# A gated linear attention with an expert layer: split first queries, one span turned by transfers, stores on two queues, and a new hand-written order

## The chip, the cores and the metric

The kernel runs on one core of a Trainium2 chip. The metric is device time in microseconds of one execution. Engines in the profile: PE (TensorE), DVE (VectorE), ACT (ScalarE), POOL (GpSimd) and SP (SyncE), which in the kernel before issues all transfers.

## The reference

```python
def _attn_ref(q, k, v, f_logit):            # each (4, 8, 768, 48)
    f = 1.0 / (1.0 + np.exp(-f_logit))
    for t in range(S):
        state = f[:, :, t, :, None] * state + np.einsum('bhd,bhe->bhde', k[:, :, t], v[:, :, t])
        y[:, :, t] = np.einsum('bhd,bhde->bhe', q[:, :, t], state)
    return y

def _moe_ref(x, w1, w2, w_out):             # x: (3072, 384), d_ff = 1024
    g = np.maximum(x @ w1, x @ w2)
    return g @ w_out
```

`y`, with the heads side by side, is the `x` of the second function. All inputs and the output are float32.

## The kernel before

**Tiling.** The 768 positions of each of 4 batches are cut into 3 windows of 256. A *span* is one window of one batch; spans 0 to 3 are the first windows, 4 to 7 the second, 8 to 11 the third. So span s needs the state that span s−4 left. A tile of an input holds one span: 128 rows, and in each row two neighbouring positions (even, odd) of all 8 heads. Each span has two halves of 64 rows, h = 0 and 1, one after the other in time.

**Work of one span.** Every step is a letter. Loads: `Lf`, `Lq`, `Lk`, `Lv`, into one of 27 `slots` (the number behind @). ScalarE makes the gates: `E`, `F` (exp and ln of the gate's input), `G`; `e` adds the two logs of a row, `C` sums them along the rows on TensorE, `Z` and `X` take exp of the sums (`dec`, `inv`). `i` and `j` put the odd gate into the even keys and queries; `K`, `Q`, `V` write scaled keys, queries and values as bf16 (`kp`, `qp`, `vb`). `t` and `u` turn keys and queries on TensorE (16 transposes each into PSUM, the queries' beside the keys'), and `U` copies the turned ones out to `trs`. `A` (two parts) multiplies turned keys and queries, `m` applies the mask while copying (`at_m`), `D` makes the state's addition, `n` and `N` update the state. `S` (two parts) adds what the old state gives to the output's banks, `y` what the masked products give; `z` is a small copy that stands between the two. `Y` copies the result out: as `xT` (features on the partitions) for most spans; for the spans in `TURNED` (6 to 10) rows stay on the partitions (`xr`, a single buffer), and `M`, a transposing transfer on SyncE's queue, makes `xT`.

**Expert layer.** max(h1, h2) = relu(h1 − h2) + h2. So `wd` = w1 − w2 (`ws`, four quarters of columns), and m2 = w2 · w_out is made once on the chip (`wc` casts w2, `wt` transposes it, `wx` copies it out, `wo` casts w_out, `wm` multiplies, `wn` copies out). `Wa`, `Wb`, `Wo` load quarters of w1, rows of w2, halves of w_out. Then for each span: `d` (four parts, 6 matmuls each) gives `wd`·x, `r` copies it with relu to `gT`, `o` (two parts by parity; three in span 11) adds m2·x (3 matmuls) and w_out·gT (8), `b` copies the result to `ob` (three buffers), `O` stores it.

**The order.** There is no scheduler at run time: the string `ORDER` is read word by word and each word calls one step. A word is the letter, the span (with the part after a point), the engine (a, v, p or s) and, behind @, a PSUM bank or a slot. Each engine runs its own instructions in this order, and waits at each for what it needs; what stands behind a waiting instruction on the same engine waits too. Up to eight transfers are in flight: the ninth is issued when the first has landed, since its semaphore is used again. Numbers such as L436 are lines of the kernel before: L114 is the helper `copy` that all plain copies share, L436 the matmuls of `d`, L461 of `o`, L292 of `A`, L387 of `D`, L314 and L323 of `S` and `y`, L503 the m2 product, L275 the transposes, L299 `m`, L261 `Q`, L258 `K`, L247 `i`, L251 `j`, L224 `e`, L511 `ws`, L404 and L406 `n`, L357 `z`, L213 `E`, L125 the input loads, L427 `M`, L475 to L482 the stores.

Of the kernel before, what the change touches and what calls it, by code (L numbers as in the profile page):

```python
# [12 lines left out]
BF16 = mybir.dt.bfloat16  # L13
# [10 lines left out]
n0.1v D1@0 m0.0v@4 S0.0@2 A1.0@6 Lk2s@25 wc2a z0v@2 m1.0v@6 A1.1@4 S0.1 y0 Lq2s@26 wc0a ws2p n1.0v  # L24
n1.1v m1.1v@4 S1.0@6 Y0.0a@2 wt2@0 Lf3s@16 E2 g5p z1v@6 N1.1v S1.1 y1 N0.1p Lv2s@17 g3p ws0v wt0@1
Y1.1a@7 wx2a@0 Y0.1v@3 wc1p Lq3s@18 Y1.0v@6 d0.2@2 F2 g1p ws3v d0.0@4 Lk3s@19 wx0a@1 wt1@0 g4v e2v
d0.3@3 ws1v C2@1 r0.1a@2 d1.2@6 Lf4s@21 wo0v wx1v@0 wo1p d0.1@5 G2 d1.3@7 r0.0v@4 d1.0@2 Lv3s@20
wo2p wo3a d1.1@3 r1.1v@6 Z2 wm0@0 X2 g6v Lk4s@22 r1.0a@2 i2v wm1@1 K2v Lf5s@23 j2v wm2@2 Q2v Lq4s@24
E3 wn1v@1 t2@4 u2@4 F3 U2.0v@4 Lf6s@12 V2p wn2a@2 wn0v@0 o0.1@1 U2.1v@5 e3p A2.1@2 Lq5s@13 b0.1.0a@1
D2@4 A2.0@6 G3 n2.0v C3@0 j3v o1.1@1 Z3 n2.1v Lk5s@0 i3v X3 Q3v o1.0@0 m2.1v@2 E4 K3p F4 m2.0v@6  # L30
# [18 lines left out]
r7.0a@4 N9.0v i10p Lv10s@24 d8.3@7 O6.2s X10 d8.1@5 r7.1a@2 K10v d8.2@6 d8.0@4 r8.1a@6 o7.1@1
r8.0a@4 j10v Q10p S9.0@2 t11@4 t10@6 z9v@2 u11@4 S9.1 y9 U11.0v@4 u10@6 U11.1v@5 o7.0@0 U10.2a@6  # L50
V11v V10v b7.1.0v@1 o8.1@4 Y9.2a@2 b7.0.0a@0 M9s D10@1 b8.1.0a@4 D11@0 O7.2s A11.0@2 A10.0@6 n11.0v
A11.1@4 m10.0v@6 o8.0@0 m11.1v@4 d9.0@6 N11.0v n10.0v d9.1@7 m11.0v@2 N10.0p d9.3@5 r9.0a@6 d9.2@4
b8.0.0v@0 O8.2s S10.0@0 r9.1a@4 S11.0@2 z10v@0 A10.1@6 z11v@2 S11.1 y11 m10.1v@6 S10.1 y10 Y11.0a@2
Y11.1a@3 o9.0@4 Y10.2a@0 M10s d11.2@5 b9.0.0v@4 d11.1@0 d11.3@1 o9.1@4 d10.1@3 b9.1.0v@4 r11.4a@5
# [7 lines left out]
TURNED = (6, 7, 8, 9, 10)  # L62


@with_exitstack
def kernel(
# [255 lines left out]
    def add_turned(s, h, n, lhs, rhs, stop):  # L322
        nc.tensor.matmul(out=banks[:, ys[s] + h, n * D:(n + 1) * D], lhsT=lhs, rhs=rhs,  # L323
                         start=(s, h) not in begun, stop=stop, skip_group_check=True)
        begun.add((s, h))

    def step_S(s, part, b):
        t = tr[s]
        if s in TURNED:
            ys[s] = b if part == 0 else ys[s]  # L330
            for j in range(NP):
# [242 lines left out]
```

## Time and profile before

| | us |
|---|---|
| median of 3 runs (139.22 to 140.53) | 140.16 |
| the profiled execution | 141.23 |
| span of the profiled execution, first to last instruction | 139.5 |
| PE busy | 119.1 |
| DVE busy | 101.7 |
| ACT busy | 79.0 |
| POOL busy | 45.3 |

In the profile, a row of an engine's time line is its start, its length, the engine, the line, the operation with the tiles it writes and reads, how many of them follow each other, and in brackets the idle time before it with what ended that. The granted clock of TensorE is given as 1.00 over the whole span. 23.59 MB are read from memory and 4.72 MB written.

### The profile page before, as it was taken

Reading aid. Unit: us, or ns where it says so; the run is one execution under the profiler, and the core shown is the slowest. Engines: PE = TensorE matmul, PEld = TensorE weight load, DVE = VectorE, ACT = ScalarE, POOL = GpSimd, SP = SyncE. Lnnn points to the kernel's source line nnn. Section 1 sums busy time; section 2 is a strip of 40 time slices with the busy share of each in tenths; the row PEclk is TensorE's granted clock in tenths of the full one; section 3 lists DMA queues with packets and bytes.
Section 4 is the critical chain, followed back from the end, with each engine's and each line's share of the span. In section 5 each row is a group of like instructions: output and inputs, shape, how many; then the busy total and the mean of one; then the engine's idle time right before and its main releaser. Section 6 shows DMA issues by size and latency. Waiting matters only on the chain. (4 is left out here: it accounts for less than half of the span.)

```text
span 139.5 us, 5551 instructions
## 1 busy us (share of the span) xinstructions
PE 119.1 (85%) x2455; PEld 89.5 (64%) x2455; DVE 101.7 (73%) x173; ACT 79.0 (57%) x120; POOL 45.3 (32%) x52
## 2 busy tenths in 40 slices
PE   0045489599999999999999699989999999999991
PEld 0024377586567687677787566776877668778671
DVE  5687798999889999989974989982642768312630
ACT  3784349665592996973983355693675814504301
POOL 5003007640538224482073096719635001000000
PEclk9999999999999999999999999999999999999999
DMA  4999999999999989999999999909899461422124
GB/s 109 271 261 296 348 332 349 369 267 251 269 265 257 271 222 273 239 248 250 247 297 222 224 274 163 288 30 96 121 260 313 130 140 34 118 56 61 57 62 164
DMA packets 59768, 29.65 MB, mean 213 GB/s; under 512 B 54368, under 2 KB 58592, under 8 KB 59744
## 3 DMA queue, kind: packets, MB, share of 16 engines
q1 hardware_dynamic: 59744, 29.30, 87.5%
q8 instruction: 19, 0.31, 1.0%
q14 instruction: 5, 0.04, 0.1%
HBM read 23.59 MB, written 4.72 MB: 203 GB/s over the span
## 5 line engine op out<-in xcount | busy, mean ns | idle before, releaser
L436 PE MATMUL banks<-xT,wd 128*128 128x256 bf16 x288 | 34.7, 273 | 2.3 <-DVE xT L114 2.0
L461 PE MATMUL banks<-wo,gT 128*128 128x384 bf16 (+1 forms) x200 | 35.3, 320 | 0.0
L436 PEld LDWEIGHTS <-wd 128*128 128x128 bf16 x288 | 27.2, 98 | 6.9 <-issue 2.3
L445 ACT ACTIVATE gT<-banks 128x1024 bf16<-128x1024 f32 (+1 forms) x20 | 19.5, 982 | 20.2 <-PE banks L436 15.7
L299 DVE TENSOR_TENSOR at_m<-banks,mask 128x1024 bf16<-128x1024 f32 x24 | 28.8, 1218 | 0.8 <-PE banks L292 0.5
L461 PEld LDWEIGHTS <-gT 128*128 128x128 bf16 x200 | 19.2, 98 | 11.8
L247 POOL TENSOR_TENSOR slots<-slots,one 128x384 f32<-128x384 f32 x8 | 8.5, 1058 | 28.1 <-DMA slots<-in_k_dram 18.3
L461 PE MATMUL banks<-m,xT 128*128 128x384 bf16 (+1 forms) x75 | 15.9, 320 | 0.0
L114 ACT COPY ob<-banks 128x384 f32<-128x384 f32 (+1 forms) x16 | 7.4, 460 | 11.9 <-PE banks L461 11.9
L114 DVE COPY trs<-banks 128x2048 bf16<-128x2048 bf16 (+1 forms) x12 | 11.9, 997 | 2.4 <-PE banks L275 2.3
L213 ACT ACTIVATE gate<-slots 128x768 f32<-128x768 f32 x12 | 10.1, 841 | 5.0 <-DMA slots<-in_f_logit_dram 5.0
L114 DVE COPY ob<-banks 128x384 f32<-128x384 f32 x9 | 5.0, 555 | 8.9 <-PE banks L461 8.9
L228 PE MATMUL banks<-e,u_inc 128*128 128x384 bf16 x12 | 4.2, 354 | 8.0 <-DVE e L224 8.0
L258 POOL TENSOR_TENSOR kp<-slots,inv 128x768 bf16<-128x768 f32 x5 | 9.6, 1913 | 3.0 <-DVE slots L247 2.9
L404 DVE TENSOR_TENSOR tmp_s<-banks,state 128x192 f32<-128x192 f32 x16 | 5.6, 352 | 6.7 <-ACT ob L114 3.9
L217 ACT ACTIVATE ell<-gate 128x768 f32<-128x768 f32 x12 | 10.1, 845 | 0.2
L292 PE MATMUL banks<-trs 48*64 48x128 bf16 x384 | 10.1, 234 | 0.0
L261 POOL TENSOR_TENSOR qp<-slots,dec 128x768 bf16<-128x768 f32 x4 | 7.3, 1817 | 8.3 <-PE banks L314 4.9
L251 DVE SCALAR_TENSOR_TENSOR slots<-gate,slots 128x384 f32<-128x384 f32 x12 | 6.6, 552 | 3.9 <-DMA slots<-in_q_dram 3.9
L114 ACT COPY trs<-banks 128x1024 bf16<-128x1024 bf16 (+1 forms) x4 | 4.8, 1227 | 7.0 <-PE banks L275 7.0
L292 PEld LDWEIGHTS <-trs 48*64 48x64 bf16 x384 | 7.5, 115 | 1.6 <-issue 1.1
L461 PEld LDWEIGHTS <-xT 128*128 128x128 bf16 x75 | 6.5, 97 | 3.2
(73 smaller groups left out, 186.3 us busy)
## 6 DMA issues: line engine op xcount, KB each, us to landing
slots<-in_f_logit_dram SPq DMA_DIRECT2D x12, 384.0 KB, 6.4
slots<-in_q_dram SPq DMA_DIRECT2D x12, 384.0 KB, 6.2
slots<-in_k_dram SPq DMA_DIRECT2D x12, 384.0 KB, 6.1
slots<-in_v_dram SPq DMA_DIRECT2D x12, 384.0 KB, 5.8
out_dram<-ob SPq DMA_DIRECT2D x6, 384.0 KB, 3.9
out_dram<-ob SPq DMA_DIRECT2D x11, 192.0 KB, 3.4
slots<-in_moe_w_dram SPq DMA_DIRECT2D x4, 384.0 KB, 8.7
slots<-in_moe_w_dram SPq DMA_DIRECT2D x3, 512.0 KB, 8.8
```

Source lines behind the costliest of these rows:

```text
L114: (nc.scalar.copy if e == "a" else engines[e].tensor_copy)(out, in_)
L213: nc.scalar.activation(flat(gate[s]), flat(loaded[s]["f"]), AF.Exp, bias=0.0, scale=-1.0)
L217: nc.scalar.activation(flat(ell[s]), flat(gate[s]), AF.Ln, bias=1.0, scale=1.0)
L247: engines[e].tensor_mul(even, even, one[s])
L251: engines[e].scalar_tensor_tensor(out=even, in0=gate[s][:, :, 1, :], scalar=1.0, in1=even, op0=ALU.add, op1=ALU.mult)
L258: engines[e].tensor_mul(pad("kp", s)[:, :, :, 0:D], by_parity(loaded[s]["k"]), both(inv[s]))
L261: engines[e].tensor_mul(pad("qp", s)[:, :, :, 0:D], by_parity(loaded[s]["q"]), both(dec[s][:, 0:HD].rearrange("p (h d) -> p h d", h=H)))
L292: nc.tensor.matmul(out=ps[h * HC:(h + 1) * HC, j % 2, par, :], lhsT=t[rows, h, 0, j, par, :], rhs=t[rows, h, 1, j].rearrange("p a t -> p ( ...
L299: nc.vector.tensor_mul(at[s][:, jj].rearrange("p r j a t -> p (r j) (a t)"), banks[:, b:b + 2, :].rearrange("p r (j x) -> p (r j) x", j=2) ...
L436: nc.tensor.matmul(out=ps[:, f], lhsT=wd[:, kt, ff * C:(ff + 1) * C], rhs=xT[g][:, kt], start=(kt == 0), stop=(kt == KT - 1))
L445: nc.scalar.activation(dst, src, AF.Relu)
L461: nc.tensor.matmul(out=ps, lhsT=lhs, rhs=rhs, start=(i == 0), stop=(i == len(terms) - 1))
```

## The change

It has four parts.

- The queries of spans 0 and 1 are scaled in two halves of four heads (`q0.0`, `q0.1`), transposed in two halves (`uq`), and copied to `trs` in two halves (`U` parts 4 and 5), apart from the keys (part 3).
- Span 11 (`BY_DMA`) has no transposes and no `U`: two transposing transfers on SyncE's queue (`Mk`, `Mq`) write `trs` straight from `kp` and `qp`, in another layout, and `A` and `S` read it through `key_t` and `query_t`. The branch for such spans inside `step_S` under `TURNED` isn't reached, as 11 is not in `TURNED`.
- `O` takes an engine. The stores of spans 7, 8, 9 and the last one of span 11 (seven transfers) are issued from ScalarE's queue, the others from SyncE's as before.
- `ORDER` is written anew from the first word to the last: order of loads, engines of many steps, banks and slots.

```diff
-Lf0s@16 g0v Lf1s@17 Lq0s@18 Lk0s@19 Lk1s@20 Lv0s@21 Lq1s@22 Wa2s E0 Wb1s F0 Lv1s@23 E1 e0v C0@0 F1
-Wb2s j0v Z0 e1v X0 Q0v G0 C1@1 Wb0s i0v X1 u0@2 G1 g2v K0v Lf2s@24 i1p t0@2 U0.0v@2 U0.1a@3 Wa0s V0v
-Z1 K1v D0@2 A0.1@0 Wa3s j1v A0.0@4 Q1v Wa1s m0.1v@0 u1@6 t1@6 Wo0s n0.0v U1.0a@6 U1.1a@7 Wo1s V1v
...
+Lf0s@16 g5p g7v g3v Lf1s@17 g2p Lk0s@18 g0p Wb2s Lq0s@19 Lq1s@20 Lv0s@21 Lf2s@22 E0 Wb0s F0 Wb1s E1
+e0v C0@0 F1 Lk1s@23 G0 X0 i0v G1 Wa1s wc2v Z0 K0v e1v Wa0s t0@0 j0v wt2@2 U0.3v@0 Lv1s@24 q0.0v C1@3
+j1v uq0.0@0 q0.1v Wa3s V0v uq0.1@0 U0.5a@0 wx2v@2 U0.4a@0 A0.1@4 Z1 Wa2s A0.0@0 m0.1v@4 X1 q1.0p E2
+Wo1s g6p q1.1v m0.0v@0 g4p uq1.1@2 uq1.0@2 U1.5a@2 wc0p D0@4 Lf3s@25 F2 n0.0v S0.0@0 Wo0s z0v@0 i1p
+n0.1v S0.1 y0 N0.1p Lq2s@26 K1v wt0@4 Y0.1a@1 wc1a U1.4v@2 ws1v t1@2 wt1@5 U1.3a@2 e2v Lk2s@16 ws0v
+C2@6 wx0a@4 A1.1@2 Y0.0v@0 Lv2s@17 V1p wx1v@5 d0.0@0 m1.1v@2 d0.1@1 Lk3s@18 ws3p A1.0@4 r0.0a@0 D1@2
+m1.0v@4 Lq3s@19 Z2 ws2p d0.3@1 G2 n1.0v X2 n1.1v S1.0@4 z1v@4 S1.1 y1 Lv3s@21 wo2v d0.2@0 Y1.0v@4
...
+j11v Z10 K10v C11@3 b6.0.0v@4 V9v Y8.2a@0 d7.3@7 d7.2@6 Z11 M8s b6.1.0a@2 Q11v d7.0@0 X11 r7.1a@6
+d7.1@1 K11p Mq11s D9@2 r7.0a@0 A9.1@4 A9.0@6 o7.0@3 O4.2s j10v Mk11s m9.1v@4 Q10p d8.3@1 O6.2s
+m9.0v@6 d8.2@0 d8.0@4 n9.0v r8.1a@0 N9.0p d8.1@5 S9.0@0 r8.0a@4 u10@6 t10@6 z9v@0 V11v S9.1 y9
+U10.2a@6 o7.1@2 Y9.2v@0 M9s b7.0.0a@3 A10.1@0 b7.1.0v@2 D11@3 A11.1@4 O5.2s A10.0@6 n11.0v O7.2a
...
 TURNED = (6, 7, 8, 9, 10)
+BY_DMA = (11,)
...
+    def step_q(s, jj, e):
+        hs = slice(4 * jj, 4 * jj + 4)
+        sums = dec[s][:, 0:HD].rearrange("p (h d) -> p h d", h=H)[:, hs]
+        engines[e].tensor_mul(pad("qp", s)[:, :, hs, 0:D], by_parity(loaded[s]["q"])[:, :, hs],
+                              sums.unsqueeze(1).to_broadcast([C, 2, 4, D]))
...
-    def transposes(s, x, b):
+    def transposes(s, x, b, js=range(NP)):
         src = pad("kpqp"[2 * x:2 * x + 2], s)
-        for j in range(NP):
+        for j in js:
...
     def step_U(s, part, e, b):
         t = tr[s] = buf("trs", s, 3, [C, 2, 2, NP, 2, HC], BF16)
+        if part > 2:
+            x, js = (0, slice(0, NP)) if part == 3 else (1, slice(2 * part - 8, 2 * part - 6))
+            src = banks16[:, b:b + 2, :].rearrange("p h (x j y) -> p h x j y", x=2, j=NP)
+            copy(e, t[:, :, x, js].rearrange("p h j a t -> p h (j a t)"),
+                 src[:, :, x, js].rearrange("p h j y -> p h (j y)"))
+            return
...
+    def whole(t):
+        return t.rearrange("p h x j a t -> p (h x j a t)").rearrange("p (x k c) -> p x k c", x=2, k=2 * NP)
+
+    def step_turn(s, x, e):
+        t = tr[s] = buf("trs", s, 3, [C, 2, 2, NP, 2, HC], BF16)
+        src = pad("kpqp"[2 * x:2 * x + 2], s).rearrange("p two h e -> p (two h e)")
+        engines[e].dma_start(out=whole(t)[:, x], in_=src, transpose=True)
+
+    def key_t(s, rows, h, j, par):
+        if s in BY_DMA:
+            return whole(tr[s])[rows, 0, NP * par + j, h * HC:(h + 1) * HC]
+        return tr[s][rows, h, 0, j, par, :]
+
+    def query_t(s, rows, h, j):
+        if s in BY_DMA:
+            return whole(tr[s])[:, 1].rearrange("p (a j) c -> p a j c", a=2)[rows, :, j, h * HC:(h + 1) * HC]
+        return tr[s][rows, h, 1, j]
...
-                        nc.tensor.matmul(out=ps[h * HC:(h + 1) * HC, j % 2, par, :],
-                                         lhsT=t[rows, h, 0, j, par, :],
-                                         rhs=t[rows, h, 1, j].rearrange("p a t -> p (a t)"),
-                                         start=True, stop=True, skip_group_check=True)
+                        nc.tensor.matmul(out=ps[h * HC:(h + 1) * HC, j % 2, par], lhsT=key_t(s, rows, h, j, par),
+                                         rhs=query_t(s, rows, h, j), start=True, stop=True, skip_group_check=True)
...
-    def step_O(g, part):
+    def step_O(g, part, e):
...
-                nc.sync.dma_start(out=dst[a], in_=obs[g][a * HC:(a + 1) * HC])
+                engines[e].dma_start(out=dst[a], in_=obs[g][a * HC:(a + 1) * HC])
...
+        "uq": lambda s, i, e, b: transposes(s, 1, b, range(2 * i, 2 * i + 2)),
+        "q": lambda s, i, e, b: step_q(s, i, e),
...
+        "Mk": lambda s, e, b: step_turn(s, 0, e), "Mq": lambda s, e, b: step_turn(s, 1, e),
```

More of the change, by code (lines that the diff above doesn't have):

```diff
@@ L26 @@
[L26 to L30, printed above, removed]
@@ L49 @@
[L49 to L54, printed above, removed]
@@ L346, in step_S @@
                     add(s, h, 2 * j + r, state_before(s, h)[rows].rearrange("p x e -> p (x e)"),
[L347 removed]
+                        D + ZP * j, query_t(s, rows, h, j), False)
     def step_z(s, b):
```

74 lines of the change are left out of this document (42 added, 32 removed).

## Prediction

> **What bounds the kernel now.** I read the page first, then a table of four stretches, then the time line of the start engine by engine, then the groups of instructions, last the transfers.
>
> ```profile
> span 139.5 us, 5551 instructions
> PE 119.1 (85%) x2455; PEld 89.5 (64%) x2455; DVE 101.7 (73%) x173; ACT 79.0 (57%) x120; POOL 45.3 (32%) x52
> ...
> DMA  4999999999999989999999999909899461422124
> ```
> ```profile
> core 0: us, PE busy (x) PEld busy (x) DVE busy (x) ACT busy (x) POOL busy (x), PEclk, DMA share, GB/s
> 0.00:25.80 25.80, 10.95 (x338) 9.39 (x338) 20.41 (x50) 15.28 (x22) 7.02 (x17) 1.00 1.07 285
> 25.80:36.30 10.50, 10.47 (x117) 8.13 (x117) 10.22 (x15) 6.53 (x11) 2.68 (x5) 1.00 1.08 283
> 36.30:136.60 100.30, 97.67 (x2008) 71.96 (x2000) 71.04 (x109) 56.84 (x91) 35.56 (x32) 1.00 0.83 189
> 136.60:139.50 2.90, 0.00 (x0) 0.00 (x0) 0.00 (x0) 0.31 (x1) 0.00 (x0) 1.00 0.36 129
> ```
>
> The reader is to see three parts. Until 25.8 us TensorE has work for 10.95 us only, while the transfers run without a break (share 1.07). From 25.8 to 136.6 us TensorE stands idle for 0.03 + 2.63 us in all: it sets the time there. The tail, 2.9 us, is the last copy and the last store. So a change can win at most about 2.7 us of idle time in the long part, what it takes off TensorE, and what it moves at the start. VectorE is the second engine to watch: 10.22 us of the 10.5 right after the start.
>
> **The start, before.** What arrives when can be read from instructions that were waiting for a transfer; they start as it lands.
>
> ```profile
> 4.45 0.84 ACT L213 ACTIVATE gate<-slots 128x768 f32<-128x768 f32 x1 [2.44 <-DMA slots<-in_f_logit_dram]
> 7.46 0.56 DVE L251 SCALAR_TENSOR_TENSOR slots<-gate,slots 128x384 f32<-128x384 f32 x1 [0.70 <-DMA slots<-in_q_dram]
> 10.60 1.15 POOL L247 TENSOR_TENSOR slots<-slots,one 128x384 f32<-128x384 f32 x1 [8.06 <-DMA slots<-in_k_dram]
> 17.37 0.56 DVE L114 CAST vb<-slots 128x768 bf16<-128x768 f32 x1 [0.81 <-DMA slots<-in_v_dram]
> 20.15 1.05 ACT L114 CAST slots<-slots 128x1024 bf16<-128x1024 f32 x1 [1.94 <-DMA slots<-in_moe_w_dram]
> 21.48 1.04 ACT L114 CAST slots<-slots 128x1024 bf16<-128x1024 f32 x1 [0.28 <-DMA slots<-in_moe_w_dram]
> 24.18 1.03 DVE L511 TENSOR_TENSOR wd<-slots 128x768 bf16<-128x768 f32 x1 [0.47 <-DMA slots<-in_moe_w_dram]
> 28.39 0.84 POOL L114 CAST wo<-slots 128x768 bf16<-128x768 f32 x1 [1.84 <-DMA slots<-in_moe_w_out_dram]
> 30.49 0.83 ACT L114 CAST wo<-slots 128x768 bf16<-128x768 f32 x1 [0.61 <-DMA slots<-in_moe_w_out_dram]
> ```
>
> The order of the loads there is f0 f1 q0 k0 k1 v0 q1 Wa2 Wb1 v1 Wb2 Wb0 f2 Wa0 Wa3 Wa1 Wo0 Wo1. They land one behind the other: f0 4.45, q0 7.46, k1 10.60, so an input tile costs about 1.5 us. Wb2 to Wb0 is 1.33 for a row block of w2. Wb0 to Wa0 (with f2) is 2.7, so a quarter of w1 is about 1.2; by 28.39 and 30.49 half of w_out is 2.1. One gap does not fit: v1 to Wb2 took 2.78 where 1.33 was due, 1.4 us more.
>
> ```profile
> 20.03 1.27 PE L314 MATMUL banks<-at_m,vb 64*64 64x128 bf16 x35
> 22.77 0.88 PE L314 MATMUL banks<-at_m,vb 64*64 64x128 bf16 x44
> 25.83 1.47 PE L436 MATMUL banks<-xT,wd 128*128 128x256 bf16 x12 [1.64 <-DVE xT L114]
> 28.51 3.43 PE L436 MATMUL banks<-xT,wd 128*128 128x256 bf16 x30
> 31.78 4.06 PE L503 MATMUL banks<-wo,slots 128*128 128x384 bf16 x24
> 35.77 0.41 PE L275 MATMUL banks<-ident,kp 64*128 64x64 bf16 x16
> 36.02 0.40 PE L275 MATMUL banks<-ident,qp 64*128 64x64 bf16 x16
> 38.24 0.43 PE L292 MATMUL banks<-trs 48*64 48x128 bf16 x16
> 38.48 0.43 PE L387 MATMUL banks<-vb,kp 64*64 64x48 bf16 x32
> ```
>
> Here TensorE takes up the expert part (d0) at 25.83, after both first spans are wholly done, and ends the product for m2 at 35.84. These two points are my marks.
>
> **The change at the start.** The new order loads f0 f1 k0 Wb2 q0 q1 v0 f2 Wb0 Wb1 k1 Wa1 Wa0 v1 Wa3 Wa2 Wo1 f3 Wo0 q2 k2 v2. With the costs above from f0 at 4.45: k0 7.4, Wb2 8.7, q0 10.2, q1 11.7, v0 13.2, f2 14.7, Wb0 16.0, Wb1 17.3, k1 18.8, Wa1 20.0, Wa0 21.2, v1 22.7, Wa3 23.9, Wa2 25.1, and Wo0 30.8, each up to 1.4 later if the unexplained gap comes back. Weights come earlier, span 1's keys 8 us later.
>
> What has to be done on VectorE is priced by these groups:
>
> ```profile
> L299 DVE TENSOR_TENSOR at_m<-banks,mask 128x1024 bf16<-128x1024 f32 x24 | 28.8, 1218 | 0.8 <-PE banks L292 0.5
> L261 DVE TENSOR_TENSOR qp<-slots,dec 128x768 bf16<-128x768 f32 x8 | 7.6, 954 | 0.2
> L258 DVE TENSOR_TENSOR kp<-slots,inv 128x768 bf16<-128x768 f32 x7 | 6.6, 945 | 1.1 <-POOL slots L247 1.0
> L224 DVE TENSOR_TENSOR e<-ell 128x384 bf16<-128x384 f32 x6 | 3.2, 541 | 0.8 <-ACT ell L217 0.8
> L511 DVE TENSOR_TENSOR wd<-slots 128x768 bf16<-128x768 f32 x3 | 2.9, 973 | 0.5 <-DMA slots<-in_moe_w_dram 0.5
> L114 DVE COPY trs<-banks 128x1024 bf16<-128x1024 bf16 x5 | 3.4, 688 | 1.5 <-PE banks L275 1.5
> L114 DVE CAST xT<-banks 128x384 bf16<-128x384 f32 x2 | 1.0, 544 | 0.0
> L404 DVE TENSOR_TENSOR tmp_s<-banks,state 128x192 f32<-128x192 f32 x16 | 5.6, 352 | 6.7 <-ACT ob L114 3.9 <-PE banks L387 2.5
> L357 DVE COPY look<-banks 128x1 f32<-128x1 f32 x4 | 0.6, 150 | 0.0
> ```
>
> The first step there that a new order can hold up is i0. It needs G0, the fifth activation on ScalarE: four of 0.84, as in the 4.45 row, and one of half the width, about 0.5, from 4.45 on, so 8.3. Then, in the order written: i0 0.54 (half a tile, as e); wc2, a cast of 1024 columns that VectorE never did before (from below the 0.69 of its 1024-column copy, from above the 1.22 of its masked product over 1024 columns; I take 1.0, near ScalarE's cast of this shape, 1.05 in the 20.15 row); K0 0.95; e1 0.54; j0 0.55; U0 0.69; q0.0 0.48; j1 0.55; q0.1 0.48; V0 0.56; wx2 0.69. That is 7.0, to 15.3. Half of Q is taken as half of 954; from below nothing is saved on it, so 0.95 at most. Then m0.1 1.22, q1.1 0.48, m0.0 1.22, n0.0 and n0.1 0.35 each, z0 0.15: 3.8, with about 1.2 of waits for TensorE between them (A0, S0), to 20.3. K1 comes next, and it is held by k1, not by VectorE: k1 at 18.8 to 20.2, then i1 on GpSimd (1.15, the 10.60 row): 20.0 to 21.4. Behind K1 stand U1 (half of 0.69, taken as 0.4), ws1 0.97, e2 0.54, ws0 0.97, Y0.0 0.54; with K1 4.4 us. So d0 can start at 24.7 to 25.8, against 25.83. That is the gain of the halves and of the earlier weights: 0 to 1.1 us.
>
> What is behind it costs more. At that point, before, span 1 was done. Now A1.0, D1, S1 and y1 are still to come: half of span 1's A (the 38.24 row less its overlap with the next) 0.3; D 0.4; S, 12 matmuls, and y1, 48, at 0.88/44 each, 1.2; in all 1.9 us of TensorE. In return wt1 and C2 are done ahead, by their columns about 0.6. And y1 waits for VectorE again: after Y0.0 come wx1 0.69, m1.1 and m1.0 2.44, n1.0 and n1.1 0.7, so 28.5 to 29.6. Until then TensorE has d0.0, d0.1, d0.3 (18 at 3.43/30, 2.06 us), A1.0, D1: 2.8 us, from 24.7, to 27.5. It idles about 1 us. After that all is dense: y1, d0.2, d1 (30 at 0.114, 3.4), the m2 product 4.06. Sum to the second mark, without C3, which is only moved: 24.7 to 25.8, plus d0 and d1 5.5, plus span 1's 1.9, plus 1.0 idle, plus 3.95 = 37.1 to 38.2. Before it was 35.84. **The start loses 1.3 to 2.3 us; I take 1.6**, nearer the lower end, as 1.4 us of gap was seen once in three such transfers. Wo0 (30.8 to 32.2) and k2 are ready before TensorE wants them.
>
> **Span 11's keys and queries by transfer.** 32 transposes leave TensorE: two groups of 16 run from 35.77 to 36.42, so 0.6 us, in the part that TensorE sets: −0.6. Two copies of 0.69 leave VectorE. Two transfers of 128x1024 come on SyncE's queue, in front of O4, O6 and M9.
>
> ```profile
> xT<-xr SPq DMA_TRANSPOSE x5, 3.8
> ...
> DMA to landing us min/median/max: 2.8/3.8/5.4
> ```
>
> The nearest rows are 768 wide: 2.8 to 5.4 us to landing, so by width 3.7 to 7.2; I take 5. In the order written K11 ends about when A9 does. From there to the first A11 TensorE has o7 (22 at 4.06/24, 3.7), d8 (24 at 0.114, 2.7), two groups of transposes 0.6, S9 and y9 about 1, half of A10 0.3: 8.3 us. That hides 5 us and even 7.2: price 0; without the cover up to 3 us. The strided moving operand of A11 has no row; the same number of columns passes, so 0 (a gain is excluded by that), at most another 0.43 for each half.
>
> **Stores on ScalarE's queue.** Seven issues leave SyncE.
>
> ```profile
> 126.73 8.13 SPq L475 DMA_DIRECT2D out_dram<-ob  x4
> 136.03 1.24 SPq L479 DMA_DIRECT2D out_dram<-ob  x2
> 136.59 0.32 ACT L114 COPY ob<-banks 128x192 f32<-128x192 f32 x1 [0.59 <-PE banks L461]
> ```
>
> The long row is mostly waits for the buffer. The two last issues fit into 1.24 us with a wait, so under 0.6 each: 4 us at most on ScalarE, which is busy 57% of the span. Behind the issues stand r9, r10 and r11; r11 is covered by o10 (22 at 0.169, 3.7 us). The last store follows its copy as now. Price 0, from above 0.6 if r10 comes late.
>
> **The long middle.** 2.63 us of idle time are spread over it, and every step is placed anew. All of it can go (−2.6) or as much again can come (+2.6). Four copies of 128x2048 leave VectorE, several half-tile products come from GpSimd; its sum hardly moves. I take −0.3, near nothing.
>
> **Sum.** +1.6 −0.6 −0.3 = +0.7 on the span, 139.5 to 140.2. The profiled execution took 141.23, 1.73 around its span, and lies 1.07 above the median of the runs, 140.16. I add the difference to the median: **140.9 us**, no change within what a measurement of this kernel tells (1%, that is 138.76 to 141.56).
>
> **The rivals.** *The middle closes up (faster).* Start at its lower end (+1.3), −0.6, and the 2.6 us of idle gone: 138.3. For it: the two queues and the freed VectorE copies lie there. Against: TensorE's 97.67 busy of 100.30 leaves nothing more. Chance 0.30.
>
> *TensorE stays slow through the new start (slower).* The rows at 20.03 and 22.77 are the same matmuls at 36 and 20 ns: TensorE ran slower by 1.8 until about 22, and changed after work from 18 on with hardly a pause. In the new order TensorE waits for k1 and the cast of Wb1 in that very stretch. If the change of speed comes only after y1, then 24 matmuls of d0 (2.7), D1, A1.0 and y1 (1.7) run 1.8 times as long: +3.5, less the 1 us that it would idle: 143.4. [...] The granted clock reads 1.00 there in both stretches, so only durations show it. Chance 0.18.
> [...]
>
> *The turned operands land late.* Mk11 stands behind Mq11 and a store, and K11 on slow GpSimd; if K11 comes late enough for the cover to fall from 8.3 to 4 us and landing takes 7, TensorE waits 3 us: 143.9. Against: the start of the transfers is early. Chance 0.06.
>
> *The stores hold ScalarE up, or the halves do nothing:* +1.5, 142.4. Chance 0.05.
>
> **How the numbers follow.** Forecast 0.41, rivals 0.30, 0.18, 0.06, 0.05. So faster by over 1% 0.30, within 0.41, slower 0.29. The range: the faster case less half a microsecond of start, 137.7, to the slow clock's 143.4. The forecast's own range is 138.8 to 141.6.
>
> **What would show it.** Right: the first d0 matmul (L436's form) at 24.7 to 25.8; the m2 product ending at 37.1 to 38.2; an idle stretch of about 1 us before y1; PE 32 instructions fewer; idle in the rest 1.5 to 3.5; no wait of A11 for a transfer. Wrong: the m2 product ending before 36.5 or after 39, idle time over 5 us after it, d0 matmuls of 0.2 us, or a last store that starts over 0.7 us after its copy.

## The result, and the profile after

The changed kernel is slower: 144.02 us median (143.19 to 145.19, 4 runs) against 139.87 us (139.22 to 140.53, 4 runs) for the kernel before beside it. The ratio is 1.030, 95% interval 1.021 to 1.040. Ratios, here and below, leave out executions that took over 1.5% longer than the fastest of the same kernel. The forecast was 140.9 us, and the range ended at 143.4.

The profiled execution of the changed kernel took 143.19 us, the fastest of its four, over a span of 141.4; that of the kernel before took 141.23, more than any of its four timed runs, over 139.5. So the two traces shown first differ by 1.9 us where the medians differ by 4.2. Both kernels were therefore profiled once more (`before_again`, 139.0; `after_again`, 142.4), and what follows rests on both pairs.

The page of the changed kernel:

```profile
span 141.4 us, 5481 instructions
PE 120.1 (85%) x2423; PEld 88.9 (63%) x2423; DVE 102.8 (73%) x174; ACT 85.6 (61%) x126; POOL 37.2 (26%) x47
...
DMA  4999999999999993999999999893789360344034
...
q8 instruction: 19, 0.31, 1.0%
```

TensorE has its 32 transposes fewer (2423 against 2455), ScalarE 6.6 us more, GpSimd 8.1 us less. The table of stretches, cut at the marks of the prediction:

```profile
core 0: us, PE busy (x) PEld busy (x) DVE busy (x) ACT busy (x) POOL busy (x), PEclk, DMA share, GB/s
0.00:24.32 24.32, 11.31 (x244) 8.82 (x244) 18.86 (x49) 13.27 (x20) 7.93 (x21) 1.00 1.06 281
24.32:38.11 13.79, 12.21 (x197) 8.80 (x191) 9.64 (x15) 9.10 (x16) 4.95 (x4) 1.00 1.12 291
38.11:45.50 7.39, 7.07 (x159) 4.49 (x160) 6.05 (x8) 6.05 (x10) 2.72 (x3) 1.00 1.24 259
45.50:53.50 8.00, 5.92 (x157) 4.03 (x156) 7.83 (x15) 4.10 (x8) 2.94 (x2) 1.00 0.96 235
53.50:137.99 84.49, 83.37 (x1683) 62.75 (x1681) 60.40 (x91) 52.72 (x73) 18.65 (x18) 1.00 0.76 178
137.99:141.40 3.41, 0.24 (x3) 0.02 (x1) 0.00 (x0) 0.32 (x1) 0.00 (x0) 1.00 0.41 134
```

The two marks lie near the forecast: the first d0 matmul comes at 24.32 us (24.7 to 25.8 was said), and the m2 product ends at 38.11 (37.1 to 38.2). The surprise is the fourth row: between 45.5 and 53.5 us TensorE is idle for 2.08 us, while VectorE is busy for 7.83 of 8.00. The time lines of TensorE, VectorE and GpSimd say why (rows of the three engines, each with its start and length):

```profile
28.42 0.24 PE L343 MATMUL banks<-trs,state 48*64 48x128 bf16 x2 [0.25 <-DVE look L394]
29.98 0.52 PE L343 MATMUL banks<-at_m,vb 64*64 64x128 bf16 x18 [0.73 <-issue]
34.05 4.06 PE L540 MATMUL banks<-wo,slots 128*128 128x384 bf16 x24
43.61 0.41 PE L282 MATMUL banks<-ident,qp 64*128 64x64 bf16 x16 [0.32 <-POOL qp L262]
52.10 0.34 PE L229 MATMUL banks<-e,u_inc 128*128 128x384 bf16 x1 [1.64 <-DVE e L225]
95.46 0.27 PE L351 MATMUL banks<-vb,at_m 64*128 64x48 bf16 x7 [0.48 <-issue]
125.66 2.56 PE L473 MATMUL banks<-xT,wd 128*128 128x256 bf16 x22 [0.48 <-DMA xT<-xr]
```
```profile
47.41 1.21 DVE L327 TENSOR_TENSOR at_m<-banks,mask 128x1024 bf16<-128x1024 f32 x1
48.53 1.42 DVE L446 TENSOR_TENSOR state<-tmp_s,dec 128x192 bf16<-128x192 f32 x2
49.88 2.17 DVE L225 TENSOR_TENSOR e<-ell 128x384 bf16<-128x384 f32 x1
51.97 0.94 DVE L115 CAST xT<-banks 128x768 bf16<-128x768 f32 x1
```
```profile
48.62 1.12 POOL L248 TENSOR_TENSOR slots<-slots,one 128x384 f32<-128x384 f32 x1 [4.16 <-ACT dec L244]
49.82 1.81 POOL L259 TENSOR_TENSOR kp<-slots,inv 128x768 bf16<-128x768 f32 x1
```

`e5` (L225) takes 2.17 us where its kind took 0.541 on average before. It starts 0.06 us after GpSimd's `K4` (L259) and ends 0.42 us behind it. By these rows it stood still for `K4`; the experiments below test that. TensorE waits 1.64 us for `e5`. In the second profile of the changed kernel `K4` runs from 49.46 to 51.27 us, and it is not `e5` that is long there (0.54) but the two state products in front of it, 0.35 us each elsewhere:

```profile
48.59 2.89 DVE L446 TENSOR_TENSOR state<-tmp_s,dec 128x192 bf16<-128x192 f32 x2
52.01 0.34 PE L229 MATMUL banks<-e,u_inc 128*128 128x384 bf16 x1 [1.49 <-DVE e L225]
```

To see where the rest goes, I take for each moment the time less the work that TensorE has done by then, that work counted at the durations that its instructions have in these traces from 25 us on, where they follow each other without a pause (256 columns about 0.114 us, as 30 in 3.43; 384 columns about 0.163 us, the distance of their starts; and so on). Call it the lag. An error in these durations shifts all kernels nearly alike, so the differences between the columns are what counts. It grows with each idle stretch and each slow one (numbers worked out from the traces, us):

| work done | before | before again | after | after again |
|---|---|---|---|---|
| 12 (at 30 to 33 us) | 18.80 | 18.47 | 20.80 | 20.86 |
| 20 | 18.80 | 18.47 | 20.84 | 20.91 |
| 32 (at 51 to 56 us) | 19.55 | 19.02 | 23.96 | 23.87 |
| 64 | 20.86 | 20.50 | 23.50 | 24.07 |
| 104 | 22.38 | 21.90 | 24.60 | 25.60 |
| 111 | 22.28 | 21.80 | 24.44 | 25.45 |

The changed kernel loses 2.0 to 2.4 us in the start and 2.4 us more between 41 and 56 us. After that the kernel before loses 1.2 to 2.2 us more than the changed one, most of it at 56 to 80 us, where it has waits of its own. The work is 0.56 us less in the changed kernel, and its tail, from TensorE's end to the end of the span, 0.25 us longer. For the first pair that is 2.0 + 2.4 − 2.2 − 0.56 + 0.25 = 1.9, for the second 2.4 + 2.4 − 1.2 − 0.56 + 0.25 = 3.3, as the spans have it (1.9 and 3.4).

### The profile page after: what moved, and what is told of

It reads as the page before. It is cut to its first block, busy times and chain, and to the rows that moved or that the text cites. A ratio compares the mean times of both kernels' runs of the same rounds, so it can differ in the third digit from the quotient of the medians.

```text
span 141.4 us, 5481 instructions
## 1 busy us (share of the span) xinstructions
PE 120.1 (85%) x2423; PEld 88.9 (63%) x2423; DVE 102.8 (73%) x174; ACT 85.6 (61%) x126; POOL 37.2 (26%) x47
## 4 chain that ended last, share of the span: by engine, by line
PE 64%; DVE 13%; DMA 10%; ACT 7%; issue 3%; POOL 1%; DVEq 0%
PE banks L498 23%; PE banks L473 20%; PE banks L343 5%; PE banks L322 4%; DMA slots<-in_v_dram 4%; PE banks L282 4%; DMA xT<-xr 3%; PE banks L351 3%; DMA slots<-in_f_logit_dram 3%; DVE e L225 3%; DVE trs L115 2%; PE banks L424 2%; ACT ell L218 2%; DVE at_m L327 2%; ACT gate L214 2%
## 5 line engine op out<-in xcount | busy, mean ns | idle before, releaser
L115 ACT COPY trs<-banks 128x2048 bf16<-128x2048 bf16 (+2 forms) x10 | 13.0, 1314 | 5.9 <-PE banks L282 5.8
L484 DVE TENSOR_SCALAR gT<-banks 128x1024 bf16<-128x1024 f32 x5 | 6.1, 1220 | 6.0 <-PE banks L473 6.0
L322 PE MATMUL banks<-trs 48*64 48x128 bf16 x384 | 9.3, 226 | 1.0 <-ACT trs L115 0.7
L262 POOL TENSOR_TENSOR qp<-slots,dec 128x768 bf16<-128x768 f32 x3 | 5.4, 1814 | 17.5 <-ACT ob L115 12.1
L259 POOL TENSOR_TENSOR kp<-slots,inv 128x768 bf16<-128x768 f32 x4 | 7.3, 1816 | 9.7 <-issue 6.8
L115 DVE COPY ob<-banks 128x384 f32<-128x384 f32 (+1 forms) x10 | 5.3, 533 | 6.1 <-PE banks L498 6.1
L225 DVE TENSOR_TENSOR e<-ell 128x384 bf16<-128x384 f32 x10 | 7.1, 712 | 2.1 <-ACT ell L218 2.1
L259 DVE TENSOR_TENSOR kp<-slots,inv 128x768 bf16<-128x768 f32 x8 | 7.9, 990 | 0.9 <-POOL slots L248 0.4
L446 POOL TENSOR_TENSOR state<-tmp_s,dec 128x192 bf16<-128x192 f32 x9 | 5.0, 564 | 13.3 <-DVE tmp_s L441 13.3
L343 PE MATMUL banks<-at_m,vb 64*64 64x128 bf16 x336 | 7.8, 231 | 0.7 <-issue 0.7
```

The source lines that it names most:

```text
L115: (nc.scalar.copy if e == "a" else engines[e].tensor_copy)(out, in_)
L225: engines[e].tensor_add(pad("e", s)[:, :, 0:D], ell[s][:, :, 0, :], ell[s][:, :, 1, :])
L259: engines[e].tensor_mul(pad("kp", s)[:, :, :, 0:D], by_parity(loaded[s]["k"]), both(inv[s]))
L322: nc.tensor.matmul(out=ps[h * HC:(h + 1) * HC, j % 2, par], lhsT=key_t(s, rows, h, j, par), rhs=query_t(s, rows, h, j), start=True, stop=T ...
L343: nc.tensor.matmul(out=to if len(rhs.shape) == 2 else to.rearrange("p (a t) -> p a t", a=2), lhsT=lhs[:, at_col + off:at_col + off + DP], ...
L484: nc.vector.tensor_relu(dst, src)
```

## The experiments

Each experiment is a kernel of its own; "changed kernel" below stands for its ten timed runs, four and six (medians 144.02 and 144.52; ratios 1.030 and 1.033).

**Both kernels a second time.** No edit.

> The kernel before, unchanged, for a second profile. If the clock's place makes the spread, its time goes with the moment at which TensorE's 128-column matmuls get fast: 138.8 to 139.5 if that is before 21 us, 140.5 to 141.5 if it is 22 us or later. If the spread has another cause, the start's rows are alike and the difference lies after 36 us.

> The kernel after, unchanged, for a second profile and a narrower median. If the clock's place is its spread, a time near 144 to 145 shows a stretch of slow matmuls between 10 and 30 us that the first profile (143.2) has not, and the same waits after 36 us. If the middle varies from execution to execution, the loss lies between 40 and 60 us.

Measured: before 140.73 (one run; the 11 beside it have the median 140.30), changed 144.52 (144.06 to 145.76), ratio 1.033 (1.028 to 1.038). The moment at which TensorE gets fast does not set the time by itself: eight transposes of w2 take 0.62 us at 21.87 us in the first profile of the kernel before and still 1.03 at 21.81 in the second, whose span is 0.5 us shorter. Of the ten timed runs of the changed kernel five have a granted clock of 0.986 to 0.988 and take 145.0 on average, five have 1.0 and take 144.0. Of 73 runs of the kernel before beside the experiments one has a clock below 0.99. A mean clock of 0.988 over 142 us is what one stretch of 3.4 us at 0.50 gives, an estimate from these two numbers and the 0.50 that the filled kernels show below. Both profiled executions of the changed kernel have 1.0, so no trace of the changed kernel shows that stretch. In these ten runs it goes with about 1 us in every second one, 0.5 us of the difference, as an estimate; no run switches it.

**The idle time of the start filled.** Spare matmuls of 128 columns into an unused bank, in front of the steps that wait until 25 us: 92 in the kernel before and 84 in the changed one (their expectations say 80), and 141 in a third kernel made from the one before. The word shown stands for 36 of them.

```diff
+    def step_h(n, b):
+        for _ in range(4 * n):
+            nc.tensor.matmul(out=banks[:, b, 0:C], lhsT=u_inc, rhs=u_inc, start=True, stop=True)
...
-C0@0
+h9.1@7 C0@0
```

> The kernel before, with 80 spare matmuls of 128 columns in the idle stretches of TensorE until 25 us (before C0, C1, t0, D0, u1, D1 and d0), into a PSUM bank that is not read; nothing else is moved. If the place at which TensorE gets fast makes the spread between executions (139.2 to 141.2), TensorE is fast from about 6 to 10 us in every execution, the spread falls under 0.7 us and the time is 138.5 to 139.5. If TensorE's speed in the start does not matter for the end, the time stays at 139.9 (within 0.5) with the same spread.

> The kernel after, with 80 spare matmuls of 128 columns in the idle stretches of TensorE until 18.5 us. If the clock's place is why its median (144.0) is 4.2 us over before while the two profiled executions differ by 1.9 only, the time falls to 141 to 142 and the spread (143.2 to 145.2) to under 1 us. If the new order loses by its waits for loads and VectorE, it stays at 143.5 to 144.5.

> [...] If filling itself costs, by queueing ahead of real work or by slowing TensorE later, 141 to 146 as with the smaller filling.

Measured: before with 92, 146.02 (142.52 to 148.47), ratio 1.022 (1.013 to 1.031, from two of its six runs); changed with 84, 147.84, ratio 1.045 (1.038 to 1.053); before with 141, 144.48, ratio 1.033 (1.028 to 1.037). All three are slower: the first two lie above every range given for them, the third lies in the range for filling that costs by itself. Stretches of the first, then of the third:

```profile
0.00:25.80 25.80, 18.48 (x401) 16.19 (x404) 19.45 (x49) 13.28 (x18) 7.06 (x17) 0.75 1.06 285
25.80:45.00 19.20, 19.14 (x260) 13.90 (x252) 16.65 (x25) 12.77 (x20) 7.53 (x7) 0.98 1.16 274
6.30:9.60 3.30, 1.45 (x30) 1.11 (x31) 2.60 (x5) 3.24 (x7) 0.00 (x0) 1.00 1.27 261
9.70:16.40 6.70, 6.19 (x148) 5.19 (x140) 5.89 (x10) 1.72 (x4) 1.16 (x1) 0.50 1.19 309
```
```profile
0.00:25.80 25.80, 18.17 (x455) 16.17 (x457) 19.16 (x49) 13.28 (x18) 6.99 (x17) 0.93 1.06 286
20.40:23.70 3.30, 3.00 (x77) 2.63 (x80) 3.06 (x6) 1.72 (x2) 1.99 (x2) 0.50 1.10 336
```

The column PEclk is 0.75 and 0.98, and 0.93. In the first kernel it is 1.00 from 6.3 to 9.6 us, with 1.45 us of work in 3.30, and 0.50 from 9.7 to 16.4, with 6.19 in 6.70; from 25.8 to 45.0 us, with 19.14 in 19.20, it is 0.98. The third has 0.50 from 20.4 to 23.7 us, with 3.00 in 3.30, and its mean over the whole execution is 0.988. What takes the clock down was not shown. But the clock is not all: 3.3 us at 0.50 cost at most 1.65 us, an estimate from these rows, and the third kernel is 4.2 slower. Its first d0 matmul comes at 28.52 us where the kernel before has it at 25.83. How much of that the spare matmuls cost by standing in front of real work was not separated. Filled like this, the start is worse than left idle.

**The changed start and the changed rest, apart.** The first takes the words of the kernel before until span 2's weights are done and the changed order from there; the second is the other way round.

```diff
 Lf0s@16 g0v Lf1s@17 Lq0s@18 Lk0s@19
...
 wn2a@2 wn0v@0
-o0.1@1 U2.1v@5 e3p A2.1@2 Lq5s@13
+g7v e3v C3@7 G3 Lq5s@13 X3 Lv4s@0 u2@2 t2@2 Z3
```

> The order of before until the m2 product is stored (span 2's transposes not yet), then all that is left in the order of after, with its turned span 11 and ScalarE stores; slots of loads given anew where the two orders clash. If the start is where the time goes (2.3 us between the marks in the profiled executions), 139.5 to 141.5. If the rest loses (waits in the middle and the tail), 142.5 to 144.5.

> The order of after until the m2 product is stored, with the split queries, then all that is left in the order of before, span 11 turned on TensorE and all stores on SyncE. If the start is where the time goes, 142 to 144. If the rest of the new order loses, 139.5 to 141.5.

Measured: 143.99 (142.65 to 145.32), ratio 1.033 (1.026 to 1.039), and 146.4 (143.75 to 146.98; too far apart for a ratio). In the first the lag is that of the kernel before until 35 us (18.6) and 23.65 at 56 us: it waits at the seam (1.58 us), at 46.5 (0.95) and at 51.5 (1.54), the last behind `V4`, whose load landed at 51.67 us. The second, changed words until `wn0a@1` and the order of before from there, waits 1.34 and 1.98 us for copies of VectorE at 56 and 63 us. So either start was lost again in the rest that follows, but partly to a seam that I had made; this pair settles nothing about the start.

**The wait near 50 us: `e5` to GpSimd.**

```diff
-N3.1v e5v Y2.2v@6 i4p
+N3.1v e5p Y2.2v@6 i4p
```

> The kernel after, with e of span 5 on GpSimd instead of VectorE. In the profile after, that instruction takes 2.17 us instead of 0.55 while GpSimd works on span 4's keys, and TensorE waits 1.63 us for it at 50.5 us. If this wait is on the path, 142.2 to 142.8. If the next wait (span 3's products and d2) takes its place, 143.7 to 144.3.

Measured: 144.3 (142.95 to 145.45), ratio 1.027 (1.022 to 1.032). The wait was replaced, as the second reading had it. What VectorE and GpSimd did then:

```profile
48.83 3.00 DVE L445 TENSOR_TENSOR state<-tmp_s,dec 128x192 bf16<-128x192 f32 x2
51.76 0.94 DVE L114 CAST xT<-banks 128x768 bf16<-128x768 f32 x1
```
```profile
48.74 0.99 POOL L247 TENSOR_TENSOR slots<-slots,one 128x384 f32<-128x384 f32 x1
49.81 1.80 POOL L258 TENSOR_TENSOR kp<-slots,inv 128x768 bf16<-128x768 f32 x1
```

With `e5` gone, the two state products that stand before it take 3.0 us beside GpSimd's `i4` and `K4`. It is not one instruction that is slow, but whichever of these comes beside `i4` or `K4`.

**The wait near 50 us: `K4` to VectorE.** First with `K4` directly behind `Y2.2`, by which it takes the even keys of span 4 before `i4` has put the gate into them, so that kernel leaves out part of the computation; then behind `i4`, as the computation has it.

```diff
-N3.1v e5v Y2.2v@6 i4p C5@0 b0.1.0v@1 b1.0.0a@2 S3.0@4 A3.0@6 Z5 K4p O0.2s
+N3.1v e5v Y2.2v@6 i4p K4v C5@0 b0.1.0v@1 b1.0.0a@2 S3.0@4 A3.0@6 Z5 O0.2s
```

> The changed kernel with one step moved: span 4's normalised keys (K4, 128x768 from two inputs) on VectorE behind the cast Y2.2 instead of on GpSimd. Theory A, a VectorE instruction with two SBUF inputs stands still while GpSimd runs one of its own two-input instructions, and TensorE's wait at 50.5 us (1.49 to 1.63 us in two profiles) is that: e5 takes 0.55 us again, TensorE's wait there falls below 0.4 us, the time falls by 0.9 to 1.5 us against the changed kernel (144.0 to 144.5), to 142.8 to 143.4. Theory B, VectorE simply has too much to do there and the wait belongs to its sum: 0.95 us more on VectorE, the wait stays at 1.2 us or more and moves to the next product, 144 to 145.

> The changed kernel with K4 on VectorE directly behind i4 in the order, i4 still on GpSimd, all of the computation as it should be. In the run with K4 ahead of i4 GpSimd did nothing beside N3.1 and e5, and 2 us were won. Theory A, only GpSimd's long product (1.81 us) matters: i4 (1.0 us) holds N3.1 up by at most 1 us, e5 starts by 49.9 and takes 0.55, TensorE's wait at 50.5 stays under 0.5 us: 142.3 to 143.2. Theory B, i4 beside N3.1 and e5 does the same as K4: the wait stays above 0.9 us and the time at 143.6 or more.

Measured: 142.24 (141.39 to 143.64), ratio 1.014 (1.008 to 1.020), and 142.95 (142.09 to 143.83), ratio 1.021 (1.016 to 1.026). The second interval ends below where that of the changed kernel begins in its six runs (1.028); that of its four runs is wider (1.021 to 1.040). VectorE and TensorE in the second:

```profile
48.84 1.40 DVE L445 TENSOR_TENSOR state<-tmp_s,dec 128x192 bf16<-128x192 f32 x2
50.16 0.54 DVE L224 TENSOR_TENSOR e<-ell 128x384 bf16<-128x384 f32 x1
50.63 0.94 DVE L114 CAST xT<-banks 128x768 bf16<-128x768 f32 x1
51.50 0.94 DVE L258 TENSOR_TENSOR kp<-slots,inv 128x768 bf16<-128x768 f32 x1
```
```profile
50.77 0.34 PE L228 MATMUL banks<-e,u_inc 128*128 128x384 bf16 x1
50.94 0.24 PE L231 MATMUL banks<-ones,e 128*128 128x2 bf16 x4
```

`e5` takes 0.54, and TensorE goes on at 50.77 without a wait, though VectorE has 0.94 us more to do. By the medians this wait is 1.1 to 1.6 us of the 4.2. The five runs of the changed kernel with a clock of 1.0 average 144.0, the six here, none below 0.997, 143.0; so 1.0 is the safer figure. The profiled execution here was the slowest of the six (143.83); it has 2.57 us of the pauses described below. `e5` itself was not too much work for VectorE; it was held up.

**Span 1's keys earlier.**

```diff
-E0 Wb0s F0 Wb1s E1 e0v C0@0 F1 Lk1s@23
+E0 Lk1s@23 Wb0s F0 Wb1s E1 e0v C0@0 F1
```

> The changed kernel with span 1's key load moved two places forward on SyncE's queue, ahead of Wb0 and Wb1. Theory A, the start is longer because span 1's keys come 8 us later than before and everything of span 1 stands behind K1: k1 lands 2.6 us earlier, near 16.1, K1 starts up to 0.9 us earlier (before that VectorE is busy with span 0), the first d0 matmul comes 0.5 to 0.9 us earlier, and the time is 143.2 to 143.8. Theory B, the rows of w2 that now land 1.5 us later (Wb0, Wb1) or VectorE's own work hold the start just as long: d0 at the same place within 0.3 us and the time 143.9 to 144.8.

Measured: 144.5 (143.36 to 145.05), ratio 1.032 (1.026 to 1.037): no gain. `K1` started at 19.64 us instead of 19.79. GpSimd's cast of Wb0, which now lands later, stood in front of `i1`:

```profile
17.60 1.04 POOL L114 CAST slots<-slots 128x1024 bf16<-128x1024 f32 x1 [0.33 <-DMA slots<-in_moe_w_dram]
18.60 1.00 POOL L247 TENSOR_TENSOR slots<-slots,one 128x384 f32<-128x384 f32 x1
```

**Single parts undone in the changed kernel.** The four stores back to SyncE's queue (alone, and with `K4` behind `i4`), and span 11 turned by TensorE.

```diff
-O7.2a
+O7.2s
-O8.2a
+O8.2s
-O9.2a
+O9.2s
-O11.2a
+O11.2s
```
```diff
-BY_DMA = (11,)
+BY_DMA = ()
...
-Mq11s
...
-Mk11s
...
-y9
+y9 t11@4 u11@4 U11.0v@4 U11.1v@5
```

> The changed kernel with the four stores O7, O8, O9 and the last quarter of O11 back on SyncE's queue. Theory A, O8's stores from ScalarE's queue made the transfer M10 (turned output of span 10) take 4.34 us where it took 2.76 before, and TensorE's wait of 0.45 to 0.53 at 126 us goes with them: 0.4 to 0.6 us faster than the changed kernel of the same call or of the calls before (144.0 to 144.5), 143.6 to 144.0. Theory B, the transfer is slow whatever queue the stores come from, since they still fall beside it: no change, 144.0 to 144.6.

> The changed kernel with K4 on VectorE behind i4 and the four stores back on SyncE's queue. In after_stores_on_sync TensorE's wait for M10 stayed at 0.49 us and the last store left no earlier, yet the median was 0.6 to 1.1 us lower. Theory A, that was the scatter of the runs (two of six with a granted clock of 0.988, the others without): 142.6 to 143.2, as after_k4_behind_i4. Theory B, the issues of 0.6 to 0.7 us on ScalarE cost something that the profile does not show: 141.8 to 142.4.

> The changed kernel with span 11's keys and queries turned on TensorE again (32 transposes behind y9, two copies on VectorE), no transfers for them. My step says 0.6 us slower than the changed kernel, 144.6 to 145.1. The rival, that those 0.6 us were lost again elsewhere (the part alone, put into the kernel before, measured 0.2 us faster with an interval of half a us to both sides), says within 0.3 us of it.

Measured: 143.44 (141.70 to 144.40), ratio 1.020 (1.012 to 1.027); with `K4`, 142.77 (142.20 to 142.92), ratio 1.017 (1.013 to 1.021), which overlaps that of `K4` alone. The transfer that turns span 10's output is as slow as with the other queue:

```profile
121.12 1.24 SPq L463 DMA_TRANSPOSE xT<-xr  x1
122.45 3.71 SPq L511 DMA_DIRECT2D out_dram<-ob  x3
```
```profile
125.52 0.70 PE L472 MATMUL banks<-xT,wd 128*128 128x256 bf16 x5 [0.49 <-DMA xT<-xr]
```

Alone, the stores' return lowers the median by 0.6 to 1.1 us, and its interval, too, ends below 1.028; on top of `K4` it lowers it by 0.2, within the scatter. The profiled executions with either queue are alike (143.13 and 143.19, the same waits of TensorE). So no mechanism is shown, and whether ScalarE's queue costs anything stays open. Span 11 on TensorE took 147.17 (146.18 to 148.46), ratio 1.048 (1.042 to 1.053), 2.6 to 3.1 us more than the changed kernel and not the 0.6 expected:

```profile
118.52 2.69 PE L473 MATMUL banks<-xT,wd 128*128 128x256 bf16 x23 [2.02 <-DMA xT<-xr]
```

I had put the two copies on VectorE in front of `Y9`, so span 9's output was turned late and TensorE waited 2.02 us for it. Its profile also has 2.59 us of the pauses described below, where the changed kernel has 1.21 and 1.49. So this run shows my placing and does not price the part.

**Single parts in the kernel before.** Span 11 by transfer; q8's load ahead of a store, and f11's, which nothing needs yet, later; both.

```diff
-t11@4
...
-u11@4
...
-U11.0v@4
...
-U11.1v@5
...
-Lv10s@24
+Lv10s@24 Mq11s Mk11s
```
```diff
-O2.2s n5.1v j7v Lq8s@25
+Lq8s@25 O2.2s n5.1v j7v
...
-Lf11s@26
...
-Lv9s@18
+Lv9s@18 Lf11s@26
```

> The kernel before with one part of the change alone: span 11's keys and queries turned by two transfers on SyncE's queue behind v10's load (issued near 104 us, A11 wants them near 112), 32 transposes and their copies gone. Theory A (my step): TensorE gives 0.6 us back and nothing waits: 0.4 to 0.8 us faster than the kernel before. Theory B, two more transfers in front of the stores of spans 4 to 6 and of the turned output of span 9 make something later: no change, or up to 0.7 us slower.

> The kernel before with two loads moved on SyncE's queue: q8 ahead of span 2's store instead of behind it, and f11, which is not needed for 25 us, behind v9. In two profiles of the kernel before VectorE stands idle 2.1 us near 76 us for q8, and TensorE loses 1.6 us in the waits of 76.5 to 78.9 behind it (0.30, 0.85, 0.38). Theory A, the wait of the queue is what costs there and nothing else is late: 1.0 to 1.6 us faster than before, near 138.9. Theory B, the next wait takes its place: within 0.4 us of before.

> The kernel before with both of its single moves: q8 ahead of span 2's store with f11 later, and span 11 turned by transfers. If each gives what its median showed (0.2 and 0.4 us) and they add up, 0.5 to 0.8 us faster than before, 139.5 to 139.8; if VectorE and the queue take it back, within 0.3 us of before. A candidate for a version that beats both.

Measured: 140.14 (ratio 1.001, 0.998 to 1.005), 139.97 (1.000, 0.997 to 1.004), and both 139.67 (0.997, 0.993 to 1.001), 12 runs each. None is shown to differ from before. The wait for q8 near 76 us is gone, and one of 0.91 us for a product of GpSimd at 61.4 us has come. By its interval, turning span 11 by transfer gained at most 0.3 us of the 0.6 that my sum gave it. The pair of both is the lowest median of all kernels here, and its interval just includes no change.

**The start of before, mended, before the changed rest.** As the first hybrid, with f5 and v4 loaded ahead of k4, q4 and f6, `C3` behind the turning of span 2, and `K4` on VectorE behind `i4` (of the loads, the order alone is shown, without slots).

```diff
-Lv3s Lk4s Lf5s Lq4s Lf6s Lq5s Lv4s Lf7s
+Lv3s Lf5s Lv4s Lk4s Lq4s Lq5s Lf7s Lf6s
...
-C3@7 G3 X3 u2@2 t2@2
+G3 u2@2 t2@2 C3@7 X3
```

> The order of the kernel before until span 2's weights are done, then the changed order, as in the earlier run of this kind (143.99), with three mends: f5 and v4 loaded ahead of k4, q4 and f6, C3 behind the turning of span 2, K4 on VectorE behind i4. Theory A, the changed start costs 2.0 to 2.4 us of the difference: with the start of before the time is that of after_k4_behind_i4 (142.95) less 2.0 to 2.4, 140.4 to 141.0. Theory B, the changed rest is paced by its loads and buffers and waits for them whatever the start: 142.2 to 143.2.

Measured: 142.43 (141.16 to 145.14), ratio 1.011 (1.006 to 1.017), against 1.021 (1.016 to 1.026) with the changed start; the two intervals just meet. So the start accounts for 0.5 us by the medians, 1.4 by the ratios, of the 2.0 to 2.4 that the lag shows at 33 us; neither reading holds whole. The profiled execution was a long one, 143.88. It lost 3.1 us in two waits:

```profile
73.54 0.24 PE L321 MATMUL banks<-trs 48*64 48x128 bf16 x1 [1.00 <-issue]
96.13 0.27 PE L350 MATMUL banks<-vb,at_m 64*128 64x48 bf16 x7 [2.12 <-issue]
```

**What "issue" is here.** These waits come in the midst of a row of like matmuls, where nothing can be awaited: 25 of 32 are done, then a pause, then 7. Counting the matmuls in front of them with the table of stretches (its first column of counts; the changed kernel up to 29.5 and 95.2 us, then the mended hybrid up to 73 us):

```profile
0.00:29.50 29.50, 15.38 (x351) 11.86 (x351) 22.93 (x55) 15.59 (x24) 12.69 (x24) 1.00 1.07 291
0.00:95.20 95.20, 77.82 (x1759) 57.72 (x1759) 79.30 (x139) 67.92 (x102) 32.54 (x43) 1.00 1.07 264
```
```profile
0.00:73.00 73.00, 56.11 (x1247) 42.52 (x1247) 63.79 (x118) 51.58 (x75) 18.93 (x30) 1.00 1.09 275
```

351, 1247 and 1759 are 7 and 4 times 128 apart. In all the traces every pause of over 0.15 us in the midst of a row that ends by "issue" stands at 95 and a multiple of 128 (also at 863, 1375, 1503 and 1887), in the kernels with spare matmuls too, where other work stands at these counts. Each matmul has a weight load beside it, so that is every 256 instructions. The page has 19 packets on the instruction queue with 0.31 MB, 16 KB each, and 2423 matmuls with as many loads are 4846 instructions, 255 for each packet. That is near the 256, but whether the pauses have to do with these packets no run shows. Of the 19 counts of this kind in the changed kernel (95 to 2399) two have such a pause in its first profile, 0.73 and 0.48 us, and the longest in any trace is 2.12. In the changed kernel the pauses are 1.21 and 1.49 us in two profiles, in the kernel before 0.52 and 0. That is 0.7 to 1.5 us between these traces. No run moves the pauses or takes them away, and what ends them is not known.

## Why the prediction was wrong, point by point

- *First d0 matmul at 24.7 to 25.8:* it came at 24.32, 0.4 earlier. Landings were as worked out: k1 came at 18.76 us where 18.8 was said, and `K1` waited for `i1` behind it until 19.79. That k1 holds `K1` was right, but moving k1 showed that the next thing in line, the cast of Wb0 on GpSimd, holds it as long.
- *m2 product ending at 37.1 to 38.2, start 1.6 us lost:* it ended at 38.11, and the lag says 2.0 to 2.4. Right in kind; the term was 0.4 to 0.8 too small. The idle 1 us before `y1` was there (0.25 and 0.73), but 0.73 of it was the pause at the count of 351 and not VectorE. How much of the start's loss is left at the end stays open between 0.5 and 1.4 us.
- *Span 11 by transfer, −0.6:* the work is 0.56 less, and no matmul waited for the turned operands. But put alone into the kernel before, the part changed the time by −0.3 to +0.6 us (its interval): less work for TensorE was not as much less time.
- *Stores on ScalarE's queue, 0:* no wait for them is seen, and the issues took 0.60 to 0.72 us each, the last 0.36; but the medians leave a cost of up to 1 us open.
- *The long middle, −0.3, "near nothing":* this is the step that failed. By the lags it is +0.2 in the first pair and +1.2 in the second (2.4 us lost until 56 us, less the 2.2 and 1.2 that the kernel before loses later). The term was priced by VectorE's sum, which "hardly moves", and not by what runs beside what: the new order moves `K4` from VectorE to GpSimd, beside `e5` and the state products. In the loss are the wait for GpSimd near 50 us (1.0 to 1.6 of the time, shown by moving `K4`), the pause at the count of 1759, at 95 us (0.48 and 0.95 in the two profiles) and 0.45 to 0.48 for span 10's turned output. TensorE's idle time from 38.11 us to its end is 3.5 us in the first profile, at the edge of the 1.5 to 3.5 that were said. The range of ±2.6 was taken from idle time alone; that the long instructions of VectorE were themselves waits did not enter it. The trace of before had the sign: its state product of 0.35 us takes 1.16 at 51.5 us, beside GpSimd's `i`:

```profile
51.54 1.16 DVE L409 TENSOR_TENSOR state<-tmp_s,dec 128x192 bf16<-128x192 f32 x1
```
```profile
51.46 1.03 POOL L247 TENSOR_TENSOR slots<-slots,one 128x384 f32<-128x384 f32 x1 [4.18 <-DMA slots<-in_k_dram]
```

- *From the span to the median:* I added a difference of spans to a median. The profiled 141.23 lay 1.36 above the median of the kernel before that counts here (139.87), and the profiled 143.19 lay 0.83 below that of the changed one: 2.0 between the profiled executions became 2.0 + 1.36 + 0.83 = 4.2. That the first pair shows so little of the loss is chance, not a term of the sum. The +0.7 is 1.2 off against the first pair of spans, 2.7 against the second and 3.5 against the medians. Of the 2.7, the middle is 1.5 (+1.2 for −0.3), the start 0.8 and the longer tail, which the sum left out, 0.25.
- *Rival, TensorE stays slow (143.4):* not in the way it was told (d0's first 12 matmuls took 1.48 us from 24.32, where they took 1.47 before). TensorE did stay slow a little longer than in one of the two traces of before: eight transposes of w2 take 1.03 us at 22.48, where the first profile of before has 0.62 at 21.87 (the second has 1.03 at 21.81). And in half of the runs the clock of 0.988 goes with 1 us more. That 143.4 lies near the measured 144.0 is luck.
- *The rivals of late operands and stores:* no such wait is seen. The one of the middle closing up: the opposite. None of the rivals had a new wait between two engines as its mechanism.

The second pair stands nearer to the medians (140.73 and 144.17 as profiled, 140.3 and 144.5 as medians of the runs beside them), and its 3.4 has the parts above; the clock may account for some 0.5 of the rest, by the estimate above. With `K4` moved the kernel is still 2.9 us slower than before, and no run takes that apart: the start is 0.5 to 1.4 of it, and the rest stays open.

## What to carry to other kernels

Price a product that moves to GpSimd by what VectorE does at that moment, too: here `e5` took 2.17 us beside `K4` and 0.54 with `K4` on VectorE. In an order written by hand, look in the profile of before for instructions that are longer than their kind, as the state product of 1.16 us where its kind takes 0.35; no idle column shows that time. And before a difference of two traces is put on a median, see where each profiled execution lies among its runs.

## What the runs showed of the hardware that was not expected

- VectorE beside GpSimd: in the two profiles of the changed kernel, VectorE ran an instruction with PSUM as a source beside a two-input product of GpSimd (for over 0.2 us) 22 and 23 times, and none took more than 0.02 us longer than the shortest of its kind. Of ten and seven with SBUF sources alone, six and five took 0.30 to 1.62 us longer. The rows of `e5` and `K4` agree, 2.17 us being the 1.75 beside `K4` and 0.42 of its own.
- Pauses at like counts: pauses of TensorE inside a row of like matmuls, 0.48 to 2.12 us in the rows above, stand at 95 and a multiple of 128 matmuls, in kernels of different orders. Their cause is open.
- The granted clock fell in the start: with 92 spare matmuls it was 1.00 from 6.3 to 9.6 us, with TensorE busy for 1.45 of 3.30 us, and 0.50 from 9.7 to 16.4, with TensorE busy for 6.19 of 6.70. The cause was not tested.
- Turning transfers vary: the one of span 10 took 4.34 us to land, with two stores issued behind it, and 2.76 before; the two of span 11 took 3.2 and 5.1. Stores alone do not explain it: that of span 9 took 2.75 with three stores behind it. The cause is open.
